# The first two attention chunks in another order, and the first full expert's row fetch moved from step 10 to steps 4 and 5

## The chip, the cores and the metric

The kernel runs on one core of one Trainium2 chip. The metric is the device time of one execution in microseconds (us). A core has a matrix engine (PE, with its weight loads listed as PEld), a vector engine (DVE), an activation engine (ACT), a general engine (POOL), and SP, which here does nothing but issue DMA transfers. Each engine works through its own instruction list in order, and a list stops at an instruction whose semaphores are not yet there; what stands behind it on that engine waits too.

## The reference

```python
# x1: mLSTM attention, batch 2, 8 heads, 768 tokens, head size 40
for t in range(S):
    m_new  = maximum(f[t] + m, i[t])
    f_stab = exp(f[t] + m - m_new); i_stab = exp(i[t] - m_new)
    C = f_stab * C + i_stab * outer(v[t], k[t])
    n = f_stab * n + i_stab * k[t]
    y[t] = sigmoid(o[t]) * (C @ q[t]) / maximum(abs(n . q[t]), 1)
# x2: 1536 tokens of width 320; 8 experts of hidden size 1024, the best two for a token
logits = x1 @ w_gate + log1p(exp(x1 @ w_noise)) * noise
for e in range(8):
    out[rows of e] += weight_of_e * (relu(x1[rows of e] @ w1[e]) @ w2[e])
# x3: a dense layer of hidden size 1536
out = (silu(x2 @ w_gate2) * (x2 @ w_val2)) @ w_out2
```

## The kernel before, in words

**Attention.** The 1536 tokens are 12 chunks of 128: chunks 0 to 5 are the first sequence, 6 to 11 the second. The gates are turned into running sums by scans on DVE (`gate_scan`, L201 to L212) and turned round on PE (`gate_cols`, L225). For chunk j, `prep_w` makes the decay weights W (ACT exponentials L269, then two triangular masks on POOL, L271), from rows that PE spreads over the partitions for chunks 0 and 1 (`gate_rows`, L238), and that SP reads back from memory for the others (tile `gbt`, L180). `scores` (PE, pS, L279) and `weigh` (DVE, L285) follow, `intra` (PE, L316), `inter` (PE, L301, which takes the state of the chunk before as Cb), `scale_k` (POOL, tile KS, L291), `state` (PE, L326), the state's sum Cs (DVE, L333) and its copy Cb (ACT, L336). `norm`, `emit_b` and `emit_a` make the chunk's output from it; `emit_a` is on POOL for chunk 0 (L354). Then `gate_t` (PE, L367; its copy xTg is ACT L369) and `gate_l` (PE, L376) give the routing logits. `warm` (L253) is a matrix product of ones that nobody reads. The sigmoid of the output gate (`sig`, ACT L985) works in place on tile x and needs another activation table than the exponentials (an ACT_TABLE_LOAD before it and one after it).

The order is written out by hand: one letter, one call. `START` is what comes before the chunk loop, `SECOND` is chunk 1's turn of that loop, `BODY` and `LAST` are the later turns. A letter of START shifted by 256 is a letter of the loop, taken for chunk 0. The engines' lists follow from this text.

**Routing.** Blocks of three chunks are routed by DVE; 24 scatters on POOL (L480) write each token's number into `slots_of`, a table in memory of which token stands in which row of which expert.

**Experts.** Experts 0 and 1 ("split": 224 rows) come first with the first sequence's tokens alone, then six "full" ones with 416 rows of both sequences, then the split ones with the second sequence's. Each expert is eight steps, so step i is expert i//8, part i%8: `mm1` (PE, ph, L655), a relu (ACT, h, L664), and two steps later `mm2` (PE, py, L692). Weights come in units: SP loads one into `stg` (L528), ACT (L545) and DVE or POOL (L546) split it into two parts wU or wV, by `pieces` in each step. Units 4 to 7 (u4 to u7) are the second split expert's; u5 is the first half of its second matrix, which mm2 of step 8 uses. `xindex` (SP, tile xi, L620) reads an expert's row numbers back from `slots_of`; `xload` (POOL, tile xgt, L612) gathers the rows by them; PE turns them (pxt, L638) and mm1 can begin. The constants `XI` and `XL` say in which step `xindex` and `xload` of the first full expert are issued:

```python
if i == XI:
    xindex(len(SPLIT), OVU)
    xindex(OVU, NU)
if i == XL:
    xload(len(SPLIT))
if i >= 4:
    pieces(RT[i], i)
```

Of the kernel before, what the change touches and what calls it, by code (L numbers as in the profile page):

```python
# [16 lines left out]
B, H, S, D = 2, 8, 768, 40  # L17
L = 128
NC = S // L
NJ = B * NC  # L20
N = B * S
DM = H * D
# [12 lines left out]
KD = 1  # L35
PA = 1
PB = 3
XI = 10


XK = (4, 5, 6)
OB = (1, 9)
XL = 10
DU = (0, 1, 2)

IW = 3
# [11 lines left out]
AG = (5, 11, 8)  # L58


START = 'gffhqkQlffffffff1cfrffff2dffsffffxoOffSffff34WKfTy5Gmfnafwfe6ffffŇŷ7ũŗŋűzųŮŭŶť'
LV = ()
SECOND = 'dGcWSdiwydddqcdKactpcdsdnmvcldecd'
BODY = 'GKcWSdiwddctpqdyacdsdnmdvclcdde'
LAST = 'iyddatdnpdmcdeslccdd'
TINY = float(np.array([0x38000000], np.uint32).view(np.float32)[0])
# [24 lines left out]
def kernel(ctx, tc, qk, kvh, og, gates, cst, wgn, noise, w1, w2, w13, w2o, out):  # L91
    nc = tc.nc
    v, s, g, pe, sy = nc.vector, nc.scalar, nc.gpsimd, nc.tensor, nc.sync
# [14 lines left out]
    def bankO(name):  # L108
        return po[0].tile([128, 512], F32, name=name, tag="O")
# [7 lines left out]
    x = per.tile([128, NJ, DX], F32, name="x")  # L117
# [54 lines left out]
    def load_kv(j):  # L172
        KV[j] = at.tile([128, H, D + DA], F32, name="kvt", bufs=3)
        sy.dma_start(KV[j], kvh[j])

    def load_gb(j):
        b, c = divmod(j, NC)
        GB[j] = at.tile([128, H, L], F32, name="gbt", bufs=3)
        src = gp[c, b * H:(b + 1) * H, :]
        sy.dma_start(GB[j].rearrange("p h t -> p (h t)"),  # L180
                     bass.AP(tensor=src.tensor, offset=src.offset, ap=[[0, 128], [1, H * L]]))
# [32 lines left out]
    def gate_cols(c0, c1, ex=True):  # L214
        r = slice(c0 * L, c1 * L)
        n = c1 - c0
        last = G_.rearrange("p (c l) -> p c l", l=L)[:, c0:c1, L - 1:L]
        v.tensor_tensor(out=bg_[:, r].rearrange("p (c l) -> p c l", l=L),
                        in0=b_[:, r].rearrange("p (c l) -> p c l", l=L),
                        in1=last.to_broadcast([16, n, L]), op=OP.add)  # L220
        p = bankO("pgc")
        for k, src in ((2, b_), (0, G_), (1, bg_)):
            for c in range(n):
                o = (c * 3 + k) * 16
                pe.transpose(p[:, o:o + 16], src[:, (c0 + c) * L:(c0 + c + 1) * L], ident[0:16, 0:16])  # L225
        pv = p[:, 0:n * 48].rearrange("p (c k h) -> p c k h", k=3, h=16)
        v.tensor_copy(bc[:, c0:c1], pv[:, :, 2])
        v.tensor_copy(eg[:, c0:c1], pv[:, :, 0:2])
        if ex:
            gate_exp(c0, c1)  # L230

    def gate_exp(c0, c1):
        s.activation(eg[:, c0:c1], eg[:, c0:c1], AF.Exp)
# [7 lines left out]
    def decays():  # L241
        s.activation(eg16, G_.rearrange("p (c l) -> p c l", l=L)[:, :, L - 1], AF.Exp)
        v.tensor_tensor(out=r16, in0=rsel[:, :, None].to_broadcast([16, 8, NC]),
                        in1=eg16[:, None, :].to_broadcast([16, 8, NC]), op=OP.mult)

    def decays_t():
        p = bankO("pdc")
        pe.matmul(p[:, 0:8 * NC], asel, r16.rearrange("p a c -> p (a c)"), start=True, stop=True)
        v.tensor_copy(dec.rearrange("p a c -> p (a c)"), p[:, 0:8 * NC])

    def warm(p, n, a=0, w=512):
        for _ in range(n):
            pe.matmul(p[:, a:a + w], ones[:, 0:128], ones[:, 0:w], start=True, stop=True)  # L253
# [20 lines left out]
    def scores(j):  # L274
        pS = [bankA("pS") for _ in range(2)]
        for p in range(4):
            for o in range(2):
                r = slice(o * 64, o * 64 + D)
                pe.matmul(pS[o][:, p * L:(p + 1) * L], QK[j][r, 1, p], QK[j][r, 0, p], start=True, stop=True)  # L279
        PS[j] = pS  # L280
# [6 lines left out]
    def scale_k(j):  # L287
        b, c = divmod(j, NC)
        if c < NC - 1:
            KS[j] = KSB[j % 2]  # L290
            g.tensor_tensor(out=KS[j][:, :, 0:D], in0=KV[j][:, :, 0:D],  # L291
                            in1=eg[:, c, 1, b * H:(b + 1) * H, None].to_broadcast([128, H, D]), op=OP.mult)
# [197 lines left out]
    def drip(k, last=False):  # L490
        spot[0] += 1
        for _ in range(k):
            if drq and (last or drq[0].__name__ != "place" or spot[0] > spot[1] + 1):
                if drq[0].__name__ == "chosen":
                    spot[1] = spot[0]
                drq.pop(0)()
# [23 lines left out]
    def wload(upto):  # L520
        while st_n[0] < min(upto, len(UN)):
            u = st_n[0]
            kind, _, src = UN[u]
            w = 1280 if kind == "V" else 1536
            ST[u] = sg_.tile([128, 1536], F32, name="stg")
            if len(src.shape) == 3:
                src = src.rearrange("p a b -> p (a b)")
            sy.dma_start(ST[u][:, 0:w], src)  # L528
            st_n[0] += 1
# [22 lines left out]
    for k in range(3):  # L552
        for src, dst, w in ((w13[k, 0], f13[k, 0], 1536), (w13[k, 1], f13[k, 1], 1536), (w2o[k], f2o[k], 1280)):
            src = src.rearrange("p a b -> p (a b)").bitcast(I32).rearrange("p (n k) -> p n k", k=2)
            for o in range(0, w, 512):
                n = min(512, w - o)
# [49 lines left out]
    def xload(n):  # L606
        C, ps_ = parts(n)
        XG[n] = mo.tile([128, 4, DX], F32, name="xgt")
        for r0, nr, m, c0 in ps_:
            a = c0 // 128  # L610
            for c in range(a, a + m):
                g.indirect_dma_start(out=XG[n][0:nr // m, c, 0:DM], out_offset=None, in_=xd[0:S] if n < len(SPLIT) else xd,  # L612
                                     in_offset=bass.IndirectOffsetOnAxis(ap=xi[0:nr // m, n, c, 0:1], axis=0))

    def xindex(n0, n1):
        C, ps_ = parts(n0)
        for r0, nr, m, c0 in ps_:
            a, p = c0 // 128, nr // m
            src = slots_of[r0:r0 + 1, :]
            sy.dma_start(xi[0:p, n0:n1, a:a + m].rearrange("p n a w -> p n (a w)"),  # L620
                         bass.AP(tensor=src.tensor, offset=src.offset, ap=[[m * SW, p], [C * SW, n1 - n0], [1, m * SW]]))
# [293 lines left out]
    def step():  # L915
# [21 lines left out]
        if f in XK and n + 1 < len(EX):  # L937
            k = XK.index(f)
            xprep(n + 1, k, k + 1)
            if k == 2 and n + 2 < len(EX) and n + 2 not in (len(SPLIT), OVU + 1):  # L940
                xload(n + 2)
# [5 lines that stand above are left out]
# [30 lines left out]
    def exp_ln():  # L977
        s.add_instruction(mybir.InstLoadActFuncSet(name=nc.get_next_instruction_name(), act_func_set_id=6,
                                                   engine=mybir.EngineType.Activation))

    exp_ln()
    pw, pib = [ps.tile([128, 512], F32, name="py", tag="Y", bufs=2) for _ in range(2)]

    def sig(b):
        s.activation(x[:, b * NC:(b + 1) * NC, 0:DM], x[:, b * NC:(b + 1) * NC, 0:DM], AF.Sigmoid)  # L985
        if b == B - 1:
            exp_ln()

    def first_w(j):
        gate_exp(j, j + 1)  # L990
        prep_w(j)

    def load_og(b):
        sy.dma_start(x[:, b * NC:(b + 1) * NC, 0:DM], og[:, b * NC:(b + 1) * NC])

    def load_gate():
        sy.dma_start(wg_t[:, :, 0:16], wgn)
# [9 lines left out]
        **ON_BOTH,  # L1007
        "r": lambda: gate_rows(0), "s": lambda: gate_rows(1),
        "x": lambda: first_w(0), "y": lambda: first_w(1),
        "o": lambda: sig(0), "O": lambda: sig(1),  # L1010
        "S": lambda: scores(0), "T": lambda: scores(1), "K": lambda: scale_k(0),
        "W": lambda: weigh(0), "a": lambda: intra(0),
        "q": lambda: load_qk(0), "Q": lambda: load_qk(1), "m": lambda: load_qk(2),
        "k": lambda: load_kv(0), "l": lambda: load_kv(1), "n": lambda: load_kv(2),
        "g": lambda: load_og(0), "h": lambda: load_og(1), "w": load_gate,
        "G": lambda: load_gb(2),
    }

    def early_piece(j):
# [7 lines left out]
        "W": (2, prep_w),  # L1027
        "S": (1, scores), "K": (1, scale_k), "w": (1, weigh),
        "i": (0, inter), "y": (0, inter_y), "a": (0, intra), "s": (0, state),
        "n": (0, norm), "e": (0, emit_a), "m": (0, emit_b),  # L1030
        "t": (-1, gate_t), "l": (-1, gate_l),
        "p": (0, early_piece), "d": (0, lambda j: drip(1)), "c": (0, lambda j: drip_s(1)),
    }

    pre = []
    for c in START:
        if c in ON_START:
# [6 lines left out]
    for j in range(NJ):  # L1044
        for c in "" if j == 0 else LAST if j == NJ - 1 else SECOND if j == 1 else BODY:
            ahead, do = ON_CHUNK[c]
            if 0 <= j + ahead < NJ:
                do(j + ahead)
        if j == 0:
            gates_s.close()  # L1050
            wv_ = [ctx.enter_context(tc.tile_pool(name="wv0", bufs=4, reuse_waits="tile"))]
            sg_ = ctx.enter_context(tc.tile_pool(name="sg", bufs=3, reuse_waits="tile"))
        if j >= KD:
            keep(j - KD)
        if j < 2:
            wload(j + 1)
        if j in BT[1:]:
            drq += route(BT[BT.index(j) - 1], j)
        if len(scat) >= 2 * NC and not pre:
            pre.append(j)  # L1060
            xindex(0, len(SPLIT))
        elif pre and j == pre[0] + PA:
            xload(0)
            xload(1)
        elif pre and j == pre[0] + PB:
            xprep(0)
# [119 lines left out]
```

## Time and profile before

| what | value |
|---|---|
| median of 3 runs | 559.98 us (558.39 to 562.45) |
| the profiled execution's own time | 560.65 us |
| its span, first to last instruction | 558.9 us |
| mean granted PE clock, as a share of full speed | 0.954 |
| PE busy | 530.8 us (95% of the span) |
| DVE, ACT, POOL busy | 376.5, 276.5, 177.1 us |

So 1.75 us of the execution lie outside the span. The profile gives for each engine when each instruction ran and, in square brackets, how long the engine had been idle before it and what it then waited for. [...]

### The profile page before, as it was taken

Reading aid. Unit: us, or ns where it says so; the run is one execution under the profiler, and the core shown is the slowest. Engines: PE = TensorE matmul, PEld = TensorE weight load, DVE = VectorE, ACT = ScalarE, POOL = GpSimd, SP = SyncE. Lnnn points to the kernel's source line nnn. Section 1 sums busy time; section 2 is a strip of 40 time slices with the busy share of each in tenths; the row PEclk is TensorE's granted clock in tenths of the full one; section 3 lists DMA queues with packets and bytes.
Section 4 is the critical chain, followed back from the end, with each engine's and each line's share of the span. In section 5 each row is a group of like instructions: output and inputs, shape, how many; then the busy total and the mean of one; then the engine's idle time right before and its main releaser. Section 6 shows DMA issues by size and latency. Waiting matters only on the chain. (4 is left out here: it accounts for less than half of the span.)

```text
span 558.9 us, 9233 instructions
## 1 busy us (share of the span) xinstructions
PE 530.8 (95%) x3333; PEld 480.6 (86%) x3335; DVE 376.5 (67%) x834; ACT 276.5 (49%) x593; POOL 177.1 (32%) x207
## 2 busy tenths in 40 slices
PE   8998698699699899999999999999999999999997
PEld 4688697689599799999999999988888888888886
DVE  6488777846379997989898967787654434443332
ACT  5376454225267586878787765545322222322221
POOL 4154757544503735253533336253000000000000
PEclk8699778969799999999999999999999999999999
DMA  8777662432647697988997768463000000010001
GB/s 250 172 279 243 213 217 75 122 119 74 200 182 264 211 296 270 323 267 300 308 316 251 274 225 284 161 202 99 0 1 23 26 1 1 1 47 1 1 0 47
DMA packets 36050, 88.67 MB, mean 159 GB/s; under 512 B 10640, under 2 KB 16944, under 8 KB 36000
## 3 DMA queue, kind: packets, MB, share of 16 engines
q1 hardware_dynamic: 30320, 75.08, 40.5%
q0 software_dynamic: 3360, 8.38, 5.2%
q10 hardware_dynamic: 2320, 4.58, 2.4%
q8 instruction: 27, 0.44, 0.4%
q14 instruction: 23, 0.19, 0.1%
HBM read 72.80 MB, written 15.21 MB: 157 GB/s over the span
## 5 line engine op out<-in xcount | busy, mean ns | idle before, releaser
L692 PE MATMUL py<-wV,h 128*128 128x320 f32 (+1 forms) x624 | 107.7, 315 | 2.3 <-ACT ysb L703 2.2
L692 PEld LDWEIGHTS py<-wV,h 128*128 128x128 f32 (+1 forms) x624 | 96.8, 188 | 3.7 <-ACT ysb L703 2.8
L655 PE MATMUL ph<-xh,wU 128*128 128x416 f32 (+1 forms) x320 | 92.8, 340 | 0.5 <-PEq L733 0.4
L585 POOL TENSOR_TENSOR cq<-cq,csg 128x512 f32<-128x512 f32 (+1 forms) x27 | 38.8, 1435 | 92.9 <-ACT cq L584 60.3
L874 PE MATMUL py<-wV,uh 128*128 128x320 f32 x288 | 63.9, 308 | 0.0
L853 DVE TENSOR_TENSOR sg<-pg,sg 128x512 f32<-128x512 f32 x36 | 24.9, 692 | 57.8 <-ACT sg L852 57.4
L655 PEld LDWEIGHTS ph<-xh,wU 128*128 128x128 f32 x320 | 60.2, 197 | 2.9 <-ACTq L733 0.7
L546 DVE TENSOR_TENSOR wU<-stg,wU 128x512 fp32r<-128x512 f32 x72 | 52.3, 752 | 6.4 <-ACT wU L545 5.8
L852 ACT ACTIVATE sg<-pg 128x512 f32<-128x512 f32 x36 | 21.6, 599 | 65.0 <-PE pg L655 59.8
L862 ACT ACTIVATE uh<-u 128x512 fp32r<-128x512 f32 x36 | 22.7, 632 | 62.1 <-DVE u L854 62.1
L655 PE MATMUL ph<-xl,wU 128*128 128x416 f32 (+1 forms) x160 | 52.5, 328 | 0.0
L874 PEld LDWEIGHTS py<-wV,uh 128*128 128x128 f32 x288 | 49.5, 188 | 2.8
L655 PE MATMUL pg<-x2h,wU 128*128 128x512 f32 x144 | 51.2, 396 | 0.0
L655 PE MATMUL pv<-x2h,wU 128*128 128x512 f32 x144 | 50.4, 391 | 0.0
L545 ACT ACTIVATE wU<-stg 128x512 fp32r<-128x512 f32 x78 | 46.4, 624 | 6.8 <-DVE yt L701 4.4
L664 ACT ACTIVATE h<-ph 128x416 fp32r<-128x416 f32 (+1 forms) x80 | 35.6, 447 | 23.3 <-PE ph L655 15.7
L874 PE MATMUL py<-wV,ul 128*128 128x320 f32 x144 | 44.4, 309 | 0.0
L546 DVE TENSOR_TENSOR wV<-stg,wV 128x640 fp32r<-128x640 f32 x42 | 38.0, 915 | 3.2 <-ACT wV L545 2.9
L655 PE MATMUL ph<-xr,wU 128*128 128x416 f32 (+1 forms) x160 | 39.3, 327 | 0.2 <-issue 0.2
L612 POOL DMA_INDIRECT xgt<-xd,xi x32 | 32.7, 1021 | 20.3 <-PEq L733 6.6
L863 DVE TENSOR_TENSOR ul<-u,uh 128x512 fp32r<-128x512 f32 x36 | 24.9, 692 | 19.9 <-ACT uh L862 19.9
L791 POOL DMA_INDIRECT gy<-yg,ig__89 x24 | 25.6, 1065 | 37.3 <-DVE x L803 15.0
(177 smaller groups left out, 1094.2 us busy)
## 6 DMA issues: line engine op xcount, KB each, us to landing
stg<-in_w_dram SPq DMA_DIRECT2D x20, 768.0 KB
stg<-in_w_dram SPq DMA_DIRECT2D x20, 640.0 KB
cw<-in_w_dram SPq DMA_DIRECT2D x18, 512.0 KB
gbt<-gp SPq DMA_DIRECT2D x10, 512.0 KB
f<-cq SPq DMA_DIRECT2D x18, 256.0 KB
stg<-f SPq DMA_DIRECT2D x6, 768.0 KB
kvt<-in_kvh_dram SPq DMA_DIRECT2D x12, 324.0 KB
QK<-in_qk_dram SPq DMA_DIRECT2D x24, 160.0 KB
```

What stands on the lines that cost most here:

```text
L545: s.activation(hi[:, c], ST[u][:, c], AF.Copy)
L546: (g if lo_pool[0] else v).tensor_tensor(out=lo[:, c], in0=ST[u][:, c], in1=hi[:, c], op=OP.subtract)
L585: g.tensor_tensor(out=q, in0=q, in1=sg, op=OP.mult)
L612: g.indirect_dma_start(out=XG[n][0:nr // m, c, 0:DM], out_offset=None, in_=xd[0:S] if n < len(SPLIT) else xd, in_offset=bass.IndirectOffse ...
L655: pe.matmul(ps_ap, a, b, start=(i == 0), stop=(i == len(seq) - 1))
L664: s.activation(h[:, 0:C], p[:, 0:C], AF.Relu)
L692: pe.matmul(yp[0:nr, 0:DM], x_, w, start=st and i == 0, stop=sp and i == 2)
L791: g.indirect_dma_start(out=y, out_offset=None, in_=yg[0:NR0] if j < NC else yg, in_offset=bass.IndirectOffsetOnAxis(ap=ig_[:, j, k:k + 1], ...
L853: v.tensor_tensor(out=sg, in0=pg, in1=sg, op=OP.mult)
L862: s.activation(uh, u, AF.Copy)
L863: v.tensor_tensor(out=ul, in0=u, in1=uh, op=OP.subtract)
L874: pe.matmul(OP_[q][a][:, 0:DM], x_[:, t], w[:, c], start=(f == 0 and i == 0), stop=(f == 11 and i == 2))
```

## The change

`XI` goes from 10 to 4 and `XL` from 10 to 5. START and SECOND are written anew: the two halves of the output gate are loaded later and apart (`g`, `H`), sig(0) moves behind chunk 1's weights and sig(1) into chunk 1's turn (letter `O` of the loop), each with a table load before and after it; chunk 0's `intra` and `state` move ahead of chunk 1's scores; `gate_cols(3, NC)`, `decays` and `decays_t` move into chunk 1's turn; there are nine fewer warm-up products. Chunk 1's decay rows come from PE in both versions. Two weight pools open one turn later, and with them the first two `wload` calls.

```diff
-XI = 10
+XI = 4
...
-XL = 10
+XL = 5
...
-START = 'gffhqkQlffffffff1cfrffff2dffsffffxoOffSffff34WKfTy5Gmfnafwfe6ffffŇŷ7ũŗŋűzųŮŭŶť'
+START = 'qkQlgmnwfffffffffff1cfffrfffxK23SffdsGfWya4ųTofeŷŗŮŭťŇŋHzűŶ'
-SECOND = 'dGcWSdiwydddqcdKactpcdsdnmvcldecd'
+SECOND = 'iSy56a7GsKtwlqffWnmefOvpff'
...
-        if b == B - 1:
-            exp_ln()
+        exp_ln()
...
-    def load_og(b):
-        sy.dma_start(x[:, b * NC:(b + 1) * NC, 0:DM], og[:, b * NC:(b + 1) * NC])
+    def load_og(a, z):
+        sy.dma_start(x[:, a:z, 0:DM], og[:, a:z])
...
-        if j == 0:
+        if j == 1:
             gates_s.close()
...
-        if j < 2:
-            wload(j + 1)
+        if 1 <= j < 3:
+            wload(j)
```

On ACT this stood at the program's start before, from chunk 0's weights (W_231) to chunk 4's (W_484); W_290, W_356 and W_405 are those of chunks 1, 2 and 3:

```order
L269 ACTIVATE W_231<-pG,bc 128x128 x8
L985 ACT_TABLE_LOAD
L985 ACTIVATE x<-x 128x6x320 x2
L978 ACT_TABLE_LOAD
...
L269 ACTIVATE W_356<-gbt,bc 128x128 x8
L336 ACTIVATE Cb_130<-Cs 64x4x41 x2
L269 ACTIVATE W_405<-gbt,bc 128x128 x8
L369 ACTIVATE xTg<-pg 128x384
L336 ACTIVATE Cb_129<-Cs 64x4x41 x2
L269 ACTIVATE W_484<-gbt,bc 128x128 x8
L369 ACTIVATE xTg<-pg 128x384
```

And this now, where W_330, W_435 and W_474 are the weights of chunks 2, 3 and 4; Cb_130 is the state for chunk 1, Cb_129 that for chunk 2:

```order
L336 ACTIVATE Cb_130<-Cs 64x4x41 x2
L985 ACT_TABLE_LOAD
L985 ACTIVATE x<-x 128x6x320
L978 ACT_TABLE_LOAD
...
L269 ACTIVATE W_330<-gbt,bc 128x128 x8
...
L336 ACTIVATE Cb_129<-Cs 64x4x41 x2
L369 ACTIVATE xTg<-pg 128x384
L269 ACTIVATE W_435<-gbt,bc 128x128 x8
L985 ACT_TABLE_LOAD
L985 ACTIVATE x<-x 128x6x320
L978 ACT_TABLE_LOAD
L269 ACTIVATE W_474<-gbt,bc 128x128 x8
```

The sigmoid moved from between the weights of chunks 0 and 1 to two places, behind the first Cb and behind chunk 3's weights, with five table loads instead of three.

On PE the new order of the start runs from chunk 0's scores (pS from QK_113) to the first inter product; W_208 is chunk 0's weight tile, KS_131 its scaled keys:

```order
L279 MATMUL pS<-QK_113 128x128 x8
...
L238 MATMUL pG<-G__122,ck 128x128 x8
...
L316 MATMUL pY<-kvt,W_208 128x123 x6
...
L326 MATMUL pY<-kvt,KS_131 64x41 x8
L279 MATMUL pS<-QK_114 128x128 x8
...
L301 MATMUL py<-Cb_130,QK_114 128x123 x3
```

Before, chunk 1's rows (the second pG) stood ahead of chunk 0's scores, chunk 1's scores ahead of chunk 0's intra, and chunk 2's scores ahead of that inter product.

On SP this is the piece at the first steps of the experts; the three `stg` loads are u5, u6 and u7, the four xi loads are `xindex` of the full experts:

```order
 L499 DMA xd<-x 128x320 x3
-L528 DMA stg<-in_w_dram 128x1280
-L528 DMA stg<-in_w_dram 128x1536
-L528 DMA stg<-in_w_dram 128x1280
 L620 DMA xi<-slots_of 128x6x24
 L620 DMA xi<-slots_of 32x6x8
 L620 DMA xi<-slots_of 128x2x8
 L620 DMA xi<-slots_of 96x2x8
+L528 DMA stg<-in_w_dram 128x1280
+L528 DMA stg<-in_w_dram 128x1536
+L528 DMA stg<-in_w_dram 128x1280
```

The four xi loads moved from behind u5, u6 and u7 to ahead of them; the gathers keep their place on POOL, behind the last scatter.

## Rows read from the trace of the kernel before

**Rows 1.** Windows: start:end, length, busy us (count) of PE, PEld, DVE, ACT, POOL, PE clock, DMA share, GB/s

```profile
10.00:23.00 13.00, 12.67 (x56) 7.95 (x58) 8.14 (x17) 8.66 (x15) 3.37 (x4) 0.50 0.71 174
...
142.00:146.00 4.00, 0.81 (x6) 0.52 (x4) 0.42 (x2) 0.32 (x1) 3.09 (x4) 1.00 0.90 283
...
147.00:152.00 5.00, 3.73 (x14) 3.22 (x15) 1.61 (x3) 2.01 (x5) 2.62 (x3) 0.50 0.40 123
...
160.00:360.00 200.00, 197.28 (x1235) 189.84 (x1234) 172.57 (x332) 141.60 (x281) 84.24 (x75) 0.99 0.79 266
```

**Rows 2.** Timeline of ACT at the start: start us, duration us, instruction, [idle before <-releaser]

```profile
10.32 1.28 ACT L985 ACT_TABLE_LOAD   x1
11.61 3.50 ACT L985 ACTIVATE x<-x 128x1920 f32<-128x1920 f32 x2
...
27.80 2.43 ACT L269 ACTIVATE W<-gbt,bc 128x128 f32<-128x128 f32 x8
...
34.14 0.49 ACT L369 ACTIVATE xTg<-pg 128x384 f32<-128x384 f32 x1 [0.84 <-PE pg L367]
35.11 0.71 ACT L336 ACTIVATE Cb<-Cs 64x164 f32<-64x164 f32 x2 [0.48 <-DVE Cs L333]
```

**Rows 3.** Timeline of POOL at the start

```profile
30.30 0.64 POOL L271 TENSOR_SCALAR_AFFINE_SELECT W<-W 128x512 f32<-128x512 f32 x1 [0.53 <-ACT W L269]
30.90 0.73 POOL L291 TENSOR_TENSOR KS<-kvt,eg 128x320 f32<-128x320 f32 x1
32.05 0.76 POOL L354 TENSOR_TENSOR x<-x,dn 128x320 f32<-128x320 f32 x1 [0.43 <-PE py L301]
```

**Rows 4.** Timeline of PE in the attention (a call's passes are counted singly)

```profile
1.52 4.45 PE L253 MATMUL py<-ones 128*128 128x512 bf16 x10 [1.52 <-POOL ones L968]
...
6.93 2.05 PE L238 MATMUL pG<-G__122,ck 16*128 16x128 f32 x16
...
11.53 3.78 PE L238 MATMUL pG<-G__122,ck 16*128 16x128 f32 x16
...
17.91 2.08 PE L279 MATMUL pS<-QK 40*128 40x128 f32 x16
...
31.84 1.92 PE L316 MATMUL pY<-kvt,W 128*128 128x123 f32 x16
...
34.04 0.67 PE L326 MATMUL pY<-kvt,KS 128*64 128x41 f32 x16
...
40.32 1.01 PE L376 MATMUL pg<-wg_t,xTg 128*128 128x128 f32 x5
...
65.25 0.88 PE L367 MATMUL pg<-ck,x 128*128 128x128 f32 x3 [4.50 <-DVE x L354]
65.92 3.48 PE L316 MATMUL pY<-kvt,W 128*128 128x123 f32 x16
```

**Rows 5.** Timeline of SP's queue in the first expert steps

```profile
112.58 0.88 SPq L528 DMA_DIRECT2D stg<-in_w_dram  x2
...
137.10 1.97 SPq L620 DMA_DIRECT2D xi<-slots_of  x4
```

**Rows 6.** Waits of SP's queue: line, releaser, us in total, times, longest us

```profile
SPq L620 <- DMA slots_of<-tok,is__88: 11.3, 2, 5.7
```

**Rows 7.** Timeline of ACT and POOL in the expert steps

```profile
133.14 1.35 ACT L545 ACTIVATE wV<-stg 128x640 fp32r<-128x640 f32 x2
...
140.07 1.17 POOL L612 DMA_INDIRECT xgt<-xd,xi  x1 [5.56 <-DMA xi<-slots_of]
```

**Rows 8.** Timeline of PE in the expert steps

```profile
136.19 1.29 PE L692 MATMUL py<-wV,h 128*128 128x320 f32 x6
...
146.50 0.48 PE L638 MATMUL pxt<-ck,xgt 128*128 128x128 f32 x1 [3.69 <-DMA xgt<-xd,xi]
148.27 1.13 PE L638 MATMUL pxt<-ck,xgt 128*128 128x128 f32 x3 [1.29 <-DMA xgt<-xd,xi]
...
152.80 0.73 PE L638 MATMUL pxt<-ck,xgt 128*128 128x128 f32 x4
```

More of the change, by code (lines that the diff above doesn't have):

```diff
@@ L1009 @@
         "x": lambda: first_w(0), "y": lambda: first_w(1),
-        "o": lambda: sig(0), "O": lambda: sig(1),
+        "o": lambda: sig(0),
         "S": lambda: scores(0), "T": lambda: scores(1), "K": lambda: scale_k(0),
@@ L1014 @@
         "k": lambda: load_kv(0), "l": lambda: load_kv(1), "n": lambda: load_kv(2),
-        "g": lambda: load_og(0), "h": lambda: load_og(1), "w": load_gate,
+        "g": lambda: load_og(0, NC), "H": lambda: load_og(NC, NJ), "w": load_gate,
         "G": lambda: load_gb(2),
@@ L1029 @@
         "i": (0, inter), "y": (0, inter_y), "a": (0, intra), "s": (0, state),
-        "n": (0, norm), "e": (0, emit_a), "m": (0, emit_b),
-        "t": (-1, gate_t), "l": (-1, gate_l),
+        "O": (0, lambda j: sig(1)), "n": (0, norm), "e": (0, emit_a), "m": (0, emit_b),
+        "f": (0, lambda j: warm(pw, 1)), "5": (0, lambda j: gate_cols(3, NC)), "6": (0, lambda j: decays()), "7": (0, lambda j: decays_t()), "t": (-1, gate_t), "l": (-1, gate_l),
         "p": (0, early_piece), "d": (0, lambda j: drip(1)), "c": (0, lambda j: drip_s(1)),
```

## The prediction

> **What bounds the kernel now.** I read four views: the windows for busy time and clock, then the timelines of ACT, POOL, PE and SP around the two places that change. In the windows the reader is to see that from 160 us on PE is the bound: 197.28 of 200 us busy at clock 0.99 [rows 1]. Nothing behind 160 is changed, so whatever PE gains or loses ahead of it reaches the end one for one, and the question is when PE gets there. In the start, PE is also busy (12.67 of 13 us from 10 to 23), but at clock 0.50 [rows 1], and much of that is warm-up products; what sets the end of this stage is when chunk 1's gate_l, at 40.32 [rows 4], lets chunk 4's scores follow, because from there on PE turns out one chunk after the other. The second place is the hand-over from the split to the full experts: PE runs out at 146.50 - 3.69 = 142.81, gets a first row block and waits again, and goes on at 148.27 [rows 8]. The rows come late because the gathers begin at 140.07, the index having been asked for at 137.10 [rows 5, 7]. That was not the place of the call in the program: SP stood 5.7 us in front of it until the scatters into slots_of had landed [rows 6].
>
> **The change, part one: the index at step 4.** What it means to remove is the wait for rows. But the last scatter still lands at 137.1, so the index is still asked for at 137.10 and answered at 140.07, and the gathers keep their place on POOL: the gain is 0. What it adds is a queue behind the wait. On SP, u5, u6 and u7 now stand behind the four xi loads. u5 and u6 were issued at 112.58 [rows 5]; now they cannot go before 137.10 + 1.97 = 139.1. Who waits: ACT splits u5 at 133.14 (two pieces, 1.35 us [rows 7]), ahead of the relu of part 7 of the second split expert, which PE's mm2 at 136.19 needs [rows 8]. Landing: u5 is 128 x 1280 words of 4 bytes, 640 KB, or 2.3 us at the 283 GB/s of the rows 142 to 146 [rows 1]; with u6 (768 KB) sharing the engines both take 5.1 us. I take 4.1, as the gathers run too: 143.2. With the two pieces and a relu (0.4, estimated from the shorter ACT rows) mm2 starts at 145.1 instead of 136.19.
>
> From there PE has 142.81 - 136.19 = 6.6 us of work left before it needs the rows, which by then (148.27) are there. So the old wait hides inside the new one, and what counts is the difference. After the old wait the clock stood at 0.50 from 147 to 152 [rows 1]; after a longer one I assume the same for some 3.5 us of the work, which costs 1.75 more: 145.1 + 6.6 + 1.75 = 153.5. The work that stood from 148.27 to 152.80 [rows 8] at the lower clock (4.5 us) is then done at the upper in about 2.6: 156.1 against 152.8, **+3.3**. Bounds: u5 lands in 2.3 us and no clock is lost, about 0 (141.4 + 1.8 + 6.6 = 149.8, then 2.6, 152.4); the whole 6.6 us at half speed and 5.1 us of landing, 146.0 + 13.2 + 2.6 = 161.8, +9, less likely since u5 goes first. I take the middle, as the old wait is its nearest row.
>
> **Part two: the start.** Removed: nine warm-up products (0.445 us each by 4.45 for ten [rows 4]), and the sigmoid of 3.50 with its two table loads ahead of chunk 1's weights (1.28 + 3.50 + 1.28 = 6.1 us [rows 2]). Added: two table loads, 2.6 us of ACT. Moved: chunk 0's intra and state to ahead of chunk 1's scores, so that the first Cb comes early; the sigmoid, in halves of 1.75, to behind the first Cb and behind chunk 3's weights. The og loads wait on SP behind QK and kvt; nobody asks for them before the first sigmoid, 20 us in, so 0 for these, and the weight pools' later opening hides behind PE likewise.
>
> When is the first Cb done? PE is in order: eleven warm-ups (1.52 to 6.4), transposes and three more (7.8), chunk 0's rows 2.05 (9.85), three more (11.2). If the clock falls there as it did, chunk 0's scores take 2.08 (13.3), two warm-ups and transposes 1.4 (14.7), chunk 1's rows 3.78 (18.5), a warm-up 0.5, intra 3.48 (22.4), state 1.1 (0.67 by the same ratio), the copy Cs 0.3 and Cb 0.71 [rows 2, 4]: 24.6. At the upper clock the same steps (scores about 1.1, half of those at 17.91, rows 2.05, intra 1.92, state 0.67 [rows 4]) end at 19.7.
>
> From there ACT's order is the path to chunk 1's gate_l: table, half sigmoid, table 4.3; chunk 2's weights 2.43 and an exponential 0.2; POOL's mask 0.64, chunk 0's emit_a 0.76 and KS of chunk 1 0.73, which all stand in one row on POOL; state of chunk 1 to the end of its Cb, 34.04 to 35.82, 1.8; xTg 0.49; chunk 3's weights 2.43; table, second half sigmoid, table 4.3; chunk 4's weights 2.43; xTg of chunk 1 0.49 [rows 2 to 4]. Sum: 21.0. emit_a waits for the sigmoid and KS for emit_a, so nothing of the first half runs beside the rest; the second sigmoid, of the second sequence, is wanted only from chunk 6 on, but stands ahead of xTg of chunk 1, and nothing covers it. So gate_l of chunk 1 comes at 24.6 + 21.0 = 45.6, **+5.3** against 40.32, or at 40.7, +0.4. I take the slow clock, because the trace shows it at 0.50 with PE busy nearly all the time and with more warm-ups than there will be [rows 1, 4].
>
> [...]
>
> [...]
>
> **Sum.** 560.65 (the profiled execution, 0.67 above the median) + 3.3 + 5.3 = 569.2, **569 us**.
>
> **Rivals.** (1) *The start keeps the upper clock.* For it: nine fewer warm-ups, work of the real kind earlier. Against it: rows 1. Then 560.65 + 0.4 + 3.3 = 564.4.
> (2) *Faster: the stall in the sixth chunk goes.* PE stands 4.50 us at 65.25 behind DVE's output step and works on at half speed, intra 3.48 where 1.92 is usual [rows 4]. It is DVE, loaded with routing, that is late there, at a time set by when POOL's scatters and PE's chunks meet. If the new phase of the start parts them, 4.5 us of waiting come back and, estimated as the intra's ratio of 1.8 over some 7 us of work, 6 us of slow clock. It decides if the start costs less than 3 us: 560.65 + 0.4 + 3.3 - 10.5 = 554; with the index delay at its lower bound, 550.6. Against it: DVE's own list is the same from chunk 3 on and is fed by PE, so it shifts with PE.
> (3) *Nothing of it is seen.* u5 lands just in time because the second sequence's routing, and the scatters, come no later while the split experts start later; the start's delay is caught up in the waits for decay rows: 558 to 563.
> (4) *More clock is lost*, in both places (the bounds above): 560.65 + 5.3 + 9 + a part of the next chunk, 576 and over.
>
> **How the numbers follow.** The forecast 0.50 (564 to 575); rival 1 0.20, rival 2 0.12, rival 3 0.11, rival 4 0.07. About 1% (5.6 us) is what a measurement of this kernel tells from no change. Slower by more needs 565.6: nearly all of the forecast and rival 4, and a little of rival 1: 0.60. Faster needs under 554.4: most of rival 2, 0.12. The same: 0.28. The range takes in rival 1, rival 3 but its lower edge, and the forecast: 557 to 575; half of rival 2 and rival 4 are left out.
>
> **What the changed profile would show.** Part one is right if SP's four xi loads are still issued only when the scatters have landed, u5's issue follows within 2 us, and PE's mm2 after the split expert's part 7 waits for a relu that stands behind ACT's pieces of u5. It is wrong if xi goes out before 130 or if PE has no new wait between 136 and 146 (shifted by the start). Part two is right if gate_l of chunk 1 starts near 45 with the second sigmoid just ahead of it on ACT, and if PE's clock is at 0.50 around 10 to 20 us. It is wrong if Cb of chunk 1 ends near 20. The forecast as a whole fails if PE's 4.50 us stall in the attention is gone, or if the delay of the start is not found again when the first expert step begins.

## The result, and the profile after

The changed kernel takes 565.35 us (median of 20 runs, 561.75 to 569.08), the one before 558.28 us in as many runs beside it (552.84 to 565.84): 1.0126 times as long, 95% interval 1.0106 to 1.0147, or 7.1 us. Ratios here and below leave out runs more than 1.5% above the fastest of their kernel. The profiled execution was one of its quicker ones: 562.23 us, span 560.5. That is only 1.6 us over the profiled execution of before, so a term cannot be read off these two profiles alone; below, stage times of fourteen profiled executions stand side by side.

**The hand-over to the full experts.** SP's queue in the changed kernel:

```profile
101.48 11.61 SPq L499 DMA_DIRECT2D xd<-x  x3
136.17 1.96 SPq L620 DMA_DIRECT2D xi<-slots_of  x4
138.22 16.88 SPq L528 DMA_DIRECT2D stg<-in_w_dram  x6
```

Nothing leaves SP between 113 and 136: it stands in front of the first index load, and u5 and u6, issued at 112.58 in [rows 5], go at 138.22, in one row with the loads behind them. The index is asked for at 136.17, 0.9 us earlier than in [rows 5], though its call stands six steps earlier. ACT's timeline shows who waits next:

```profile
142.09 1.36 ACT L545 ACTIVATE wV<-stg 128x640 fp32r<-128x640 f32 x2 [10.06 <-DMA stg<-in_w_dram]
143.36 0.34 ACT L664 ACTIVATE h<-ph 128x224 fp32r<-128x224 f32 x1
```

and PE's timeline of the same place what comes of it:

```profile
135.73 0.38 PE L655 MATMUL ph<-xr,wU 128*128 128x224 f32 x2
143.75 0.90 PE L692 MATMUL py<-wV,h 128*128 128x320 f32 x2 [7.64 <-ACT h L664]
...
152.04 0.66 PE L638 MATMUL pxt<-ck,xgt 128*128 128x128 f32 x4
...
154.52 0.66 PE L638 MATMUL pxt<-ck,xgt 128*128 128x128 f32 x4
```

The relu (L664) has nothing to do with u5, but it stands behind u5's two pieces in ACT's list, and PE behind the relu. The wait for rows of [rows 8] is gone (pxt at 152.04 has no bracket) only because PE arrives later than the rows. The second group of pxt stands at 154.52, at 152.80 in [rows 8].

**The start.** PE in the changed kernel, from chunk 0's scores to chunk 1's gate_l:

```profile
10.62 1.16 PE L279 MATMUL pS<-QK 40*128 40x128 f32 x16
...
14.94 3.17 PE L316 MATMUL pY<-kvt,W 128*128 128x123 f32 x16
...
24.78 0.50 PE L225 MATMUL pgc<-ck,bg__124 16*128 16x16 f32 x3 [1.76 <-DVE bg__124 L218]
25.21 3.64 PE L316 MATMUL pY<-kvt,W 128*128 128x123 f32 x16
...
36.24 2.08 PE L279 MATMUL pS<-QK 40*128 40x128 f32 x16
...
43.50 1.01 PE L376 MATMUL pg<-wg_t,xTg 128*128 128x128 f32 x5
```

gate_l of chunk 1 starts at 43.50, at 40.32 in [rows 4]. ACT beside it, with the two sigmoids and chunk 4's weights:

```profile
19.27 0.70 ACT L336 ACTIVATE Cb<-Cs 64x164 f32<-64x164 f32 x2 [3.45 <-DVE Cs L330]
19.99 1.28 ACT L985 ACT_TABLE_LOAD   x1
21.28 1.80 ACT L985 ACTIVATE x<-x 128x1920 f32<-128x1920 f32 x1
...
35.84 1.80 ACT L985 ACTIVATE x<-x 128x1920 f32<-128x1920 f32 x1
...
41.30 0.47 ACT L369 ACTIVATE xTg<-pg 128x384 f32<-128x384 f32 x1
```

The first Cb ends at 19.97, and xTg of chunk 1 at 41.77, 1.7 us before gate_l takes it. So in this execution ACT did not end last. The windows (columns as in [rows 1]) show what did:

```profile
10.00:23.00 13.00, 12.59 (x121) 10.86 (x121) 11.16 (x25) 7.35 (x18) 3.62 (x5) 0.87 0.58 171
...
24.00:36.00 12.00, 10.05 (x50) 7.83 (x51) 5.33 (x15) 8.29 (x25) 5.30 (x8) 0.52 0.97 250
36.00:48.00 12.00, 12.00 (x105) 11.20 (x105) 7.44 (x19) 10.18 (x24) 4.54 (x6) 0.77 0.83 289
...
160.00:360.00 200.00, 196.81 (x1239) 188.73 (x1238) 172.67 (x335) 140.11 (x281) 84.03 (x75) 1.00 0.79 268
```

The clock was mostly at the upper level, 1.00, up to 23 us this time (0.92 from 10 to 15 us, 0.95 from 17 to 23), with a dip to 0.50 from 15 to 17 us, in which chunk 0's intra took 3.17 us. From 24 to 36 it was at the lower level, 0.50 (mean 0.52), just where it was at 1.00 before, as this window of the kernel before shows:

```profile
24.00:36.00 12.00, 11.23 (x126) 9.50 (x128) 8.13 (x26) 7.14 (x24) 5.41 (x8) 1.00 0.75 217
```

In the changed kernel, PE has no gap from 36 to 48 (12.00 of 12 us busy): its own list, partly at half speed (clock 0.50 from 36 to 41 us), sets gate_l. Behind 160 nothing has changed.

### The profile page after: what moved, and what is told of

The parts are those of the page before. It is cut to its first block, busy times and chain, and to the rows that moved or that the text cites. A ratio compares the mean times of both kernels' runs of the same rounds, so it can differ in the third digit from the quotient of the medians.

```text
span 560.5 us, 9203 instructions
## 1 busy us (share of the span) xinstructions
PE 529.8 (95%) x3323; PEld 482.0 (86%) x3326; DVE 378.7 (68%) x834; ACT 278.9 (50%) x595; POOL 176.0 (31%) x207
## 5 line engine op out<-in xcount | busy, mean ns | idle before, releaser
L545 ACT ACTIVATE wU<-stg 128x512 fp32r<-128x512 f32 x78 | 46.5, 625 | 8.5 <-DVE yt L701 5.7
L664 ACT ACTIVATE h<-ph 128x416 fp32r<-128x416 f32 (+1 forms) x80 | 35.5, 446 | 19.2 <-PE ph L655 17.3
L874 PE MATMUL py<-wV,ul 128*128 128x320 f32 x144 | 44.4, 309 | 0.0
L545 ACT ACTIVATE wV<-stg 128x640 fp32r<-128x640 f32 x46 | 33.2, 733 | 12.1 <-DMA stg<-in_w_dram 10.1
```

What stands on the lines that cost most here:

```text
L545: s.activation(hi[:, c], ST[u][:, c], AF.Copy)
L664: s.activation(h[:, 0:C], p[:, 0:C], AF.Relu)
L874: pe.matmul(OP_[q][a][:, 0:DM], x_[:, t], w[:, c], start=(f == 0 and i == 0), stop=(f == 11 and i == 2))
```

## The experiments

Theory A is the prediction's: the index part costs by u5 and u6 standing behind the wait for the scatters, the start costs by itself, and the two add up. Theory B: the index part is the whole loss. Theory C: the start is. Each ratio is against runs of the kernel before made beside it; 1% is 5.6 us.

**e1, the index change alone.**

```diff
-XI = 10      (of before)
+XI = 4
-XL = 10
+XL = 5
```

> The kernel before with the index change alone (XI 4, XL 5; the start untouched). Theory A (both parts cost: u5 behind the wait for the scatters on SP, and the start): 2 to 4 us slower than before, PE idle some 7 us ahead of the mm2 that follows part 7 of the second split expert, ACT's wait for u5 of some 9 us, and no wait of PE for the gathered rows. Theory B (the index alone is the whole loss, the start's delay is caught up before the experts): 6 to 8 us slower. Theory C (the start alone is the loss): within 1 us of before.

Measured: 1.0056 (1.0021 to 1.0092), 3.1 us. PE's waits from 130 to 160 us (line, releaser, us in total, times, longest):

```profile
PE py L692 <- ACT h L664: 8.8, 1, 8.8
```

There is no wait for rows among them. C falls, since the interval excludes no change, and B, since it ends at 5.2 us.

**e2 and e12, the new start alone** (one kernel, measured at two times, on two chips).

```diff
-XI = 4       (of after)
+XI = 10
-XL = 5
+XL = 10
```

> The changed kernel with XI and XL back at 10: the new start alone. Theory A: 3 to 5 us slower than before, chunk 1's gate_l near 43.5 us and the last scatter 0.5 to 3 us later than before's 133.44. Theory B: within 1 us of before. Theory C: 6 to 8 us slower.

> The new start alone once more, since its first interval (0.9971 to 1.0049) leaves open whether it costs anything by itself. If the start's delay of 3 to 8 us at gate_l of chunk 1 reaches the end in part, the ratio is 1.003 to 1.008; if it is given back on the way, within 0.3% of before. In its profile the last scatter should stand some 2 to 6 us later than before's 133.44, and the time from the last scatter's issue to the first index load should be near 1.1 us after its end, as in the new starts so far, or 2.5 as in before.

Measured: 1.0010 (0.9971 to 1.0049) and 1.0086 (1.0049 to 1.0123). The two intervals only touch; their mean, 1.005 or 2.7 us, is the best figure there is, and that the start costs something is likely rather than settled. The last scatter starts at 139.72 and 138.18, 6.3 and 4.7 us later than before; 0.5 to 3 were expected for e2, 2 to 6 for e12. In both profiles gate_l of chunk 1 is late, first e2, then e12:

```profile
47.52 1.01 PE L376 MATMUL pg<-wg_t,xTg 128*128 128x128 f32 x5
```

```profile
46.50 1.01 PE L376 MATMUL pg<-wg_t,xTg 128*128 128x128 f32 x5
```

and PE waits for rows again, for less than the 5.0 us of [rows 8]; first e2, then e12:

```profile
PE pxt L638 <- DMA xgt<-xd,xi: 2.8, 2, 1.8
PE pxt L638 <- DMA xgt<-xd,xi: 2.8, 2, 1.9
```

The last scatter's issue ended at 140.68 in e2 and the index was asked for at 141.84, 1.2 us later; in e12 1.1. In before and e1 it was 2.7 and 2.5. So the hand-over gives about 1.5 us back in these two. The new start alone does not decide it: e11, which has the same start, needs 2.1 us, and e7, another new start, 2.9. Why the scatter lands sooner in some versions was not found.

**e3 and e11, the index load one or two weight loads later.**

```diff
-XI = 4       (of after)         -XI = 4
+XI = 5       (e3)               +XI = 7       (e11)
-XL = 5                          -XL = 5
+XL = 6                          +XL = 8
```

> The changed kernel with XI 5 and XL 6: of the three weight loads only u5 stands ahead of the four index loads again, u6 and u7 stay behind them. If u5 alone makes the new wait, this is as the new start alone (3 to 4 us under the changed kernel); if u6 does it too, since ACT splits it ahead of the relus for the next mm2, PE waits some 5 us two matrix groups later and the time is within 1.5 us of the changed kernel.

> The changed kernel with XI 7 and XL 8: u5 and u6 stand ahead of the four index loads again, u7 alone behind them. If the loss of the index part is u5 and u6 coming late, it is gone (as the new start alone, within 0.4% of before, PE waits for the gathered rows and not for a relu); if the u7 wait counts too, half of it is left.

Measured: 1.0032 (0.9996 to 1.0068) and 1.0059 (1.0024 to 1.0095). With u5 alone ahead of the index, PE's wait falls from 7.64 to 5.51 us and moves one mm2 on:

```profile
150.76 2.24 PE L692 MATMUL py<-wV,h 128*128 128x320 f32 x6 [5.51 <-ACT h L664]
```

With u5 and u6 ahead there is no wait for a relu any more, and the wait for rows is back:

```profile
PE pxt L638 <- DMA xgt<-xd,xi: 6.3, 2, 5.6
```

So the waits rank as expected (u5, then u6, then nothing). The times say less. Both lie under the changed kernel's 1.0126, but their intervals overlap that of its second measurement (e8 below, 1.0087), and the two lie within what e2 and e12 differ by. e11 was expected within 0.4% of before and is not: its index left 2.1 us after the last scatter's issue instead of 1.2, and its wait for rows is 6.3 us against 2.8 in e2.

**e4, the index loads from POOL.**

```diff
-            sy.dma_start(xi[...], ...)
+            (g if n0 >= len(SPLIT) else sy).dma_start(xi[...], ...)
```

> The changed kernel with the four index loads issued by POOL, behind its last scatter, instead of SP: nothing on SP waits for the scatters, the index itself can come no earlier. Theory A: as the new start alone, 3 to 5 us slower than before, with u5 issued near 113 and PE's wait for rows back at some 6 us. Theory B: within 1 us of before. If the earlier call has a gain of its own, it is under the new start alone.

Measured: 1.0092 (1.0049 to 1.0134), above e2 but not clear of e12 (1.0086). The undoing has a price of its own in the trace. POOL's timeline:

```profile
137.23 0.97 POOL L480 DMA_INDIRECT slots_of<-tok,is__88  x1 [0.21 <-issue]
...
139.62 2.86 POOL L620 DMA_DIRECT2D xi<-slots_of  x4 [1.33 <-DMA slots_of<-tok,is__88]
146.01 1.04 POOL L612 DMA_INDIRECT xgt<-xd,xi  x1 [3.54 <-PE ph L655]
```

u5 was out at 115.84, but the four loads take POOL 2.86 us to issue (SP 1.96), and the first gather follows 6.4 us after the first of them instead of 2.9 in e2. The profile puts the gather's wait down to a PE product, which had ended some 0.5 us before, so what released it is not settled. The rows come later, and PE waits 4.7 us for them. The run does not tell the theories apart: it takes away the wait for u5 and brings a wait for rows instead.

**e8, the changed kernel again.**

```diff
(no edit: after.py as it is)
```

> The changed kernel itself, on the chip of this call, for comparison with the partial versions: 1.0126 is to come again within 0.4%. Its second profile shows how far the start and the hand-over to the full experts differ between executions: with the clock falling at 10 us gate_l of chunk 1 is at 47 to 49 us instead of 43.5, and the end some 3 us later.

Measured: 1.0087 (1.0054 to 1.0121). Its profile is a longer execution, span 569.3, and shows the other end of the start, two windows and PE's gate_l:

```profile
10.00:23.00 13.00, 13.00 (x76) 10.72 (x76) 8.64 (x16) 3.26 (x12) 3.76 (x5) 0.50 0.44 145
24.00:36.00 12.00, 12.00 (x80) 10.64 (x77) 5.72 (x19) 7.16 (x14) 3.34 (x5) 0.50 0.89 233
```

```profile
48.84 1.01 PE L376 MATMUL pg<-wg_t,xTg 128*128 128x128 f32 x5
```

PE is busy every microsecond of both windows at clock 0.50, the first Cb ends at 23.82, and gate_l of chunk 1 is at 48.84. The same program had it at 43.50. Its end is 8.8 us later than in the first profile, where some 3 were expected.

**e5, e6, e7, what makes the start late.** All three have XI and XL at 10. e5 puts both sigmoids at the place of the first, e6 takes the five warm-ups of chunk 1's turn away, e7 puts both sigmoids between the weights of chunks 0 and 1. e5 and e7 also load the second half of the output gate (`H`) earlier.

```diff
     def sig(b):                                   (e5, e7)
-        s.activation(..., AF.Sigmoid)
-        exp_ln()
+        if b == 0:
+            for b in range(B):
+                s.activation(..., AF.Sigmoid)
+            exp_ln()
-START = '...gmnwf...ųTofe...ŋHz...'
+START = '...gmnwHf...ųTofe...ŋz...'               (e5)
+START = '...gHmnwf...fffxoK23...ųTfe...ŋz...'     (e7)
-SECOND = 'iSy56a7GsKtwlqffWnmefOvpff'
+SECOND = 'iSy56a7GsKtwlqWnmeOvp'                  (e6)
```

> The new start alone (XI and XL at 10), with both sigmoids one behind the other at the place of the first: one table pair less, none between chunk 3's and chunk 4's weights; the second half of the gate is loaded earlier for it. If the second sigmoid stands on the path to chunk 1's gate_l, as predicted, gate_l comes some 2.5 us earlier than in the new start (43.5 to 48.9 in the profiles so far) and the time is about 2 us under it. If PE's own list is what ends last there (it had no gap ahead of gate_l in the changed kernel), there is no gain, and 1.8 us more ahead of chunk 2's weights may cost that.

> The new start alone without the warm-up products of chunk 1's turn of the loop (five between gate_l of chunk 0 and chunk 3's scores). If PE's list at the lower clock sets gate_l of chunk 1, it comes up to 2 us earlier, until ACT's chain through the second sigmoid ends last; if ACT's chain does, or if the clock falls further without them, no gain or a loss of 1 to 2 us.

> The new start alone with both sigmoids and one table pair put back between the weights of chunks 0 and 1, where ACT stands idle in the new order, and both gate loads ahead of chunk 2's. If the sigmoids behind the first Cb make the delay, gate_l of chunk 1 comes 4 to 8 us earlier than in the new start (at 37 to 42) and the time is 3 to 5 us under the new start, at or under the kernel before. If the slow clock of PE in its first 25 us makes it, gate_l comes within 2 us of the new start's. A rival within it: the 2 MB of gate land late, chunk 1's weights with them, and half of the gain is lost.

Measured: 1.0040 (1.0004 to 1.0076), 0.9995 (0.9958 to 1.0031), 0.9976 (0.9935 to 1.0018), with gate_l of chunk 1 at 44.8, 44.6 and 43.2, against 47.5 and 46.5 in e2 and e12. Each is some microseconds earlier than those two, but one profile each does not show a gain: the changed start by itself ranges from 43.5 to 48.9. None brings it back to 40.3. e7's time is where the sigmoids' place as the cause would put it, and its gate_l lies between what that and the clock as the cause would give; which of the two it is stays open. In e7 no table load or sigmoid is left behind the first Cb, and PE still works through its list at half speed (clock 0.50 from 20 to 35 us, 0.58 from 35 to 40):

```profile
26.62 3.64 PE L316 MATMUL pY<-kvt,W 128*128 128x123 f32 x16
...
35.39 2.32 PE L253 MATMUL py<-ones 128*128 128x512 bf16 x5
37.64 1.91 PE L279 MATMUL pS<-QK 40*128 40x128 f32 x16
...
43.17 1.01 PE L376 MATMUL pg<-wg_t,xTg 128*128 128x128 f32 x5
```

In e4 and e11, which have the sigmoids as in after but a mean clock of 0.76 from 10 to 45 us, PE does wait for ACT at gate_l, 1.04 us:

```profile
44.35 1.01 PE L376 MATMUL pg<-wg_t,xTg 128*128 128x128 f32 x5 [1.04 <-ACT xTg L369]
```

In after, e2, e3, e8 and e12, with means from 0.50 to 0.71, gate_l waits for nothing; in after, e2 and e8 xTg was there 1.7 to 2.1 us before gate_l took it. So two chains of nearly one length run beside each other: ACT's through the sigmoids, which ended last in the two profiles with the better clock, and PE's own list, which did in the other five.

**e9 and e10, nine warm-ups back.** To e2 and to e7, behind chunk 1's scores (e10 has one more in place of the o that moved).

```diff
-START = '...ųTofe...'
+START = '...ųToffffffffffe...'     (e9; e10 the same without the o)
```

> The new start alone with the nine warm-up products back, in one row behind chunk 1's scores, where PE is at the lower clock in most profiles. They cost PE 4.2 us by themselves. If the missing warm-ups are why PE stays at half speed through chunk 1 and 2 (15 to 45 us), the clock comes back by some 30 us, intra of chunk 1 takes 1.9 instead of 3.6, and gate_l of chunk 1 is not later than the new start's 43.5 to 48.9; if the clock doesn't depend on them, gate_l comes up to 4 us later and the time rises with it.

> The same nine warm-ups in the version with both sigmoids early (0.9976 of before): there PE's list at the lower clock was all that was left ahead of gate_l of chunk 1 (43.2). If they bring the clock back, gate_l comes at 40 or earlier and the time falls under that version, below before; if not, gate_l comes at 45 to 47.

Measured: 1.0065 (1.0022 to 1.0107) and 1.0133 (1.0085 to 1.0182). gate_l is at 48.3 in both: 0.8 and 1.8 us later than in e2 and e12, and 5.1 later than in e7. In e10 a call of scores took 2.08 us ahead of the ten products (at 20.17) and 1.16 behind them (at 26.63), so the clock rose in between, and then PE waited:

```profile
22.18 3.18 PE L253 MATMUL py<-ones 128*128 128x512 bf16 x10
31.25 0.50 PE L225 MATMUL pgc<-ck,bg__124 16*128 16x16 f32 x3 [2.99 <-DVE bg__124 L218]
```

The clock, 0.80 from 20 to 30 us, was at 0.54 from 30 to 45. Put back at this place, the warm-ups do not bring gate_l forward. In e10 they cost time against e7 (0.9976); e9 is not clear of e2 and e12. Other places for them were not tried.

No version is shown to beat the kernel before. The ratios of e6 and e7 lie just under 1, but their intervals hold 1, and their medians over all twelve runs (564.2 and 564.1 us) lie above the 562.9 of before beside them.

## Why the prediction held, point by point

**The forecast.** 569 us was 8.35 over the profiled execution of before; the medians moved by 7.1 in the first comparison and by 0.87% (4.9 us) in e8. The direction held, and so did the two places, the second less firmly. The parts are consistent with adding up: e1 (3.1 us) and the mean of e2 and e12 (2.7) make 5.8.

**Part one, the index.** The gain of 0 held: the index is asked for when the scatters have landed, whatever the step. The chain held link by link, with sizes: u5 issued at 138.2 (139.1 forecast), landed by 142.09 (143.2), mm2 at 143.75 (145.1), first pxt at 152.04 (153.5), second at 154.52 (156.1), each about 1 to 1.6 us early, as the scatters landed 0.9 us earlier and u5 took less than assumed. The loss was put at 3.3; e1 has 3.1. From the first product of the split experts to the first of the full experts' ordinary steps, the profiles with the index at step 4 need 44.9 (after), 45.6 (e8) and 46.6 (e1), those with it at step 10 need 43.5 (before), 42.0 (e2) and 41.9 (e12): 3.1 with the old start, 3.3 with the new. Single profiles of this stage scatter, though: the five with the index at step 10 and yet other starts (e5, e6, e7, e9, e10) need 40.5 to 43.7, and e3, e4 and e11 need 44.0 to 44.5.

**Part two, the start.** gate_l of chunk 1 was put at 45.6. Seven profiles with this start (after, e2, e3, e4, e8, e11, e12) have it at 43.5, 47.5, 48.9, 44.4, 48.8, 44.4 and 46.5, mean 46.3; the old start at 40.3 and 42.1 (before, e1). Place and size held there, but two steps under them did not. The link of the sum that failed is that nothing covers the second sigmoid: PE's list at the lower clock covers it in five of the seven, where gate_l waits for nothing (xTg was ready 1.7 to 2.1 us early in after, e2 and e8). That the sum came out near all the same is luck: the slow clock lasts longer than was taken, 0.50 still from 36 to 41 us in after and from 40 to 45 in e8. And the first Cb was put at one of two times, 24.6 or 19.7: it ends at 19.97 in after, at 23.82 in e8, and between them, at 22.51, in e6, whose START is the same.

In after's own profile two of the prediction's signs of being wrong are there: the first Cb ends near 20, and hardly anything of the delay is left when the first expert step begins (114.60, against 114.31 before). The delay shows in the other six profiles, where that step begins at 116.8 to 121.4.

What was mis-sized is what reaches the end: 5.3 at gate_l was carried through at full size. The first product of the split experts comes 3.5 us later than with the old start (mean of the seven, 118.8, against 114.3 and 116.2), and the hand-over gives back 1.5 more; about 2 to 3 us are left, which is what e2 and e12 measured in the mean. Of the 1.6 us lost between gate_l and the split experts, some 0.5 come back by chunk 2's gate_l, and some 0.9 between the gate_l of chunks 3 and 5: 18.2 and 18.3 us with the old start, 17.2 to 17.4 in six of the seven, 18.1 in e2.

**The rivals.** The first (the upper clock is kept) was half true of one execution, after's: its first Cb was there at 19.97, in spite of the dip, but the clock then fell from 24 us on (0.52 to 36), and gate_l was 3.2 late, not 0.4. The second (the stall in the sixth chunk goes) came only in small: PE's wait there is 4.50 before and 4.49 in e2, but 2.87 in after, e3, e8 and e12. It stands between the gate_l of chunks 3 and 5, so its gain is at most the 0.9 us named above, not 10.5. The third (nothing is seen) is excluded by the interval. The fourth (both places lose more clock) is e8's start alone.

## What to carry to other kernels

Calling a load earlier in a program only helps if what it waits for comes earlier; otherwise it stands in its queue, and what stands behind it there is late: here the index left SP at 136.17 us with its call six steps earlier, at 137.10 before, and u5 at 138.22 in place of 112.58. Read the queue for what is behind the moved wait, then the consumers of that, in the order of their own lists: here a weight load, a conversion, and a relu that shares nothing with them but ACT.

When two lists of nearly one length meet, expect that taking work off one brings only the distance to the other, here 1.04 us (e4, e11) on ACT's side and 1.7 to 2.1 us (after, e2, e8) on PE's. And a single profile of a program with a moving clock is one draw: sizes should be taken between stages of several executions, not from the ends of two.

## What the runs showed of the hardware that was not expected

The clock of the same start differs between executions: from 10 to 45 us the mean is 0.71 in after and 0.50 in e8 and e3, with gate_l of chunk 1 between 43.5 and 48.9. PE was busy 13.00 of 13 us at 0.50 in e8, with warm-up products among its work. The lower clock was thus no sign here that PE had gaps just then.

Four plain loads from POOL took 2.86 us to issue, and the first gather followed 3.54 us later (e4); from SP it was 1.96 and about 0.9 in e2. The table load was 1.28 us each time in before, after, e2 and e5 to e8, and in after the sigmoid began at once (19.99 and 21.28).

From the end of the last scatter's issue to the index load that waits for it, 1.1 to 1.2 us passed in nine of the thirteen profiles with the index on SP, and 2.1 to 2.9 in the other four (before, e1, e7, e11); the cause was not found.
